# Reordering the opening of an attention-then-FFN kernel, filling TensorE's idle start with products of zeros, and spreading batch 1's attention over the w3 blocks

## The chip, the cores and the metric

The kernel runs on one core of one Trainium2 chip. The metric is the device time of one execution in microseconds (us); lower is better. Profiles are of one execution, and their times count from the start of its span.

## The reference

Eight batches of eight heads, sequence length 576, head width 64. Attention without softmax (cosFormer): rectified queries and keys are multiplied by a cosine and a sine of the position, which makes 128 features of 64 channels; then two products and a division. The result, laid out as 4608 tokens of 512 channels, goes through a feed-forward part with two input products multiplied with each other and two output matrices without a function between them.

```python
def phi(x, c, s):
    r = np.maximum(x, 0.0)
    return np.concatenate([r * c, r * s], axis=-1)
q_p = phi(q, cos_w, sin_w)
k_p = phi(k, cos_w, sin_w)
kv = np.einsum('bhsf,bhsd->bhfd', k_p, v)
z = np.sum(k_p, axis=2)
num = np.einsum('bhsf,bhfd->bhsd', q_p, kv)
den = np.einsum('bhsf,bhf->bhs', q_p, z)[..., None] + 1e-06
x = num / den                    # then laid out as (4608, 512)
...
a = x @ w1
b = x @ w2
h = a * b @ w3
out = h @ w_out
```

## The kernel before

**Attention of one batch.** The 576 positions are held as five chunks: four of 128 rows and one of 64 (`ROWS`). For each chunk `c` of batch `b`:

- `prep_k` and `prep_q` call `features` (L169 and after): VectorE makes the cosine half (L170), ScalarE the sine half (L172), of all eight heads.
- `prep_v` (L184) copies v beside a column of ones into `va`, on VectorE for batches 0 and 1, on POOL (GpSimd) for later ones.
- `q_tr` transposes the query features of the eight heads on TensorE into a PSUM buffer `pst` (L214), and VectorE copies them to `qpT` (L215).
- `kv_chunk` adds the chunk's product of key features and `va` into one PSUM tile (L200). After the fifth chunk ScalarE and VectorE copy one half each to `kvs` (L205, L206).
- `num` multiplies `qpT` by `kvs` (L225); VectorE adds, inverts and multiplies (L229, L230, L232) to give `xblk`.
- `x_tr` transposes `xblk` on TensorE (L251), and ScalarE copies it to `xT` (L252), the input of the FFN.

`num` of batch 0, chunks 0 to 3, uses the pool `ps_first` (two buffers), which is closed before the FFN starts; all later `num` and `kv_chunk` use one buffer, `pnum`. The transposes (`q_tr`, `x_tr`, `w3_tr`) share two `pst` buffers.

**FFN.** Nine tiles `t` of 512 tokens. `ffn_groups(t)` is a generator: sixteen groups of four products with w1 (L291, copied by ScalarE, L294) and w2 (L298, multiplied in by VectorE, L300) in turn, then four output slices of eight products (L305) with `w34b`, copied by ScalarE (L310) and stored by SP (L312). It yields after each w1 or w2 group and twice in each output slice, and after yield `g` the units in `slots[g]` are issued.

**w3 and w_out.** As there is nothing between them, `w34b` = w3 @ w_out is computed once, inside tile 0, in slot 15. For each of eight row blocks `jp`, `w3_tr` transposes a block of w3 (L142); VectorE copies five eighths (L144) and ScalarE, behind it, three (L145) into one of two `w3T` buffers; `w34_mm` makes eight products (L152), and ScalarE copies the result (L154). `w3_tr(jp + 1)` is issued ahead of `w34_mm(jp)`.

**Order.** The schedule is manual: each engine executes its instructions in the order in which the program issues them, and waits at the head of its queue. `spread` deals a list of units evenly over a range of slots. `attention_units(b, done)` gives a batch's attention without the feature part; `done` says how many `q_tr` were issued elsewhere. In slot 15 of tile 0, `extra` puts work of batch 1 behind the named blocks: key features behind block 3, query features behind block 5, three `q_tr` behind block 6, the v copies behind block 7; the rest is spread over slots 16 to 23. Tile 1 carries the features of batches 2 and 3 and the attention of batch 2, and so on.

**Loads.** All loads are issued by POOL in program order at the start: keys of batch 0 (`ks`), queries (`qs`), v (`vs`), w1, w2, w_out, w3 and batch 1 in alternation, batch 2. Batch 3's loads are issued in slot 20 of tile 0 and wait for batch 1's buffers. Each q, k or v load has two halves (L93, L95).

Of the kernel before, what the change touches and what calls it, by code (L numbers as in the profile page):

```python
# [10 lines left out]
FP32 = mybir.dt.float32  # L11
BF16 = mybir.dt.bfloat16
I32 = mybir.dt.int32
ALU = mybir.AluOpType
ACTF = mybir.ActivationFunctionType

P = 128
H, S, D = 8, 576, 64
F = 2 * D
NCH = 5  # L20
# [3 lines left out]
def _trig_tables(nc, pool):  # L24

    s_i = pool.tile([P, NCH], I32, name="s_i")
    nc.gpsimd.iota(s_i[0:64, :], pattern=[[1, 5]], base=0, channel_multiplier=5)
    nc.gpsimd.iota(s_i[64:128, :], pattern=[[1, 5]], base=320, channel_multiplier=4)
    th = pool.tile([P, NCH], FP32, name="th")
    nc.vector.tensor_copy(out=th[:], in_=s_i[:])  # L30
    nc.vector.tensor_scalar_mul(out=th[:], in0=th[:], scalar1=math.pi / 2 / S)
    t2 = pool.tile([P, NCH], FP32, name="t2")
    nc.vector.tensor_mul(out=t2[:], in0=th[:], in1=th[:])

    def poly(outt, coefs):
        nc.vector.tensor_scalar_mul(out=outt[:], in0=t2[:], scalar1=float(coefs[0]))
        for c in coefs[1:-1]:
            nc.vector.scalar_tensor_tensor(out=outt[:], in0=outt[:], scalar=float(c), in1=t2[:],
                                           op0=ALU.add, op1=ALU.mult)

    cosv = pool.tile([P, NCH], FP32, name="cosv")
    poly(cosv, [-1 / 3628800, 1 / 40320, -1 / 720, 1 / 24, -1 / 2, 1.0])
    nc.vector.tensor_scalar_add(out=cosv[:], in0=cosv[:], scalar1=1.0)
    sinv = pool.tile([P, NCH], FP32, name="sinv")
    poly(sinv, [-1 / 39916800, 1 / 362880, -1 / 5040, 1 / 120, -1 / 6, 1.0])
    nc.vector.scalar_tensor_tensor(out=sinv[:], in0=sinv[:], scalar=1.0, in1=th[:],
                                   op0=ALU.add, op1=ALU.mult)
    return cosv, sinv
# [3 lines left out]
def kernel(  # L52
# [11 lines left out]
    nc = tc.nc  # L64
# [6 lines left out]
    const = ctx.enter_context(tc.tile_pool(name="const", bufs=1))  # L71
# [9 lines left out]
    ps_first = first.enter_context(tc.tile_pool(name="ps_first", bufs=2, space=bass.MemoryType.PSUM))  # L81
# [7 lines left out]
    def load(b, which):  # L89
        for name in which:  # L90
            src = {"k": k, "v": v, "q": q}[name]
            t = ld.tile([P, H, NCH, D], BF16, name=name + "s")
            nc.gpsimd.dma_start(out=t[0:64, :, :, :].rearrange("p h j d -> p h (j d)"),  # L93
                                in_=src[b, :, 0:320, :].rearrange("h (p j) d -> p h (j d)", j=5))
            nc.gpsimd.dma_start(out=t[64:128, :, 0:4, :].rearrange("p h j d -> p h (j d)"),  # L95
                                in_=src[b, :, 320:S, :].rearrange("h (p j) d -> p h (j d)", j=4))
            raw[b, name] = t
# [10 lines left out]
        nc.gpsimd.dma_start(out=w3b[:, jp, :], in_=moe_w3[ts(jp, P), :])  # L108

    load(0, "k")  # L110
    cosv, sinv = _trig_tables(nc, const)
    load(0, "q")
    identb = const.tile([P, P], BF16, name="identb")
# [45 lines left out]
    def feat_of(b):  # L159
        if b not in feat:  # L160
            feat[b] = (
                phi.tile([P, NCH, H, F], BF16, name="kp"),
                phi.tile([P, NCH, H, F], BF16, name="qp"),
                va_bufs[b % 2],
            )
        return feat[b]

    def features(dst, src, c):
        R = ROWS[c]  # L169
        nc.vector.tensor_scalar(out=dst[:R, c, :, 0:D], in0=src[:R, :, c, :], scalar1=0.0,  # L170
                                scalar2=cosv[:R, c:c + 1], op0=ALU.max, op1=ALU.mult)
        nc.scalar.activation(out=dst[:R, c, :, D:F], in_=src[:R, :, c, :], func=ACTF.Relu,  # L172
                             scale=sinv[:R, c:c + 1], bias=0.0)

    def prep_k(b, c):
        features(feat_of(b)[0], raw[b, "k"], c)

    def prep_q(b, c):
        features(feat_of(b)[1], raw[b, "q"], c)

    def prep_v(b, c):
        R = ROWS[c]
        eng = nc.vector if b < 2 else nc.gpsimd
        eng.tensor_copy(out=feat_of(b)[2][:R, c, :, 0:D], in_=raw[b, "v"][:R, :, c, :])  # L184
# [3 lines left out]
    def att_of(b):  # L188
        if b not in att:
            att[b] = {"qpT": phi.tile([P, H, S], BF16, name="qpT"), "x": {}}  # L190
        return att[b]

    def kv_chunk(b, c):
        R = ROWS[c]
        kp, qp, va = feat[b]
        if c == 0:
            att_of(b)["kv"] = ps_att.tile([P, 2, 512], FP32, name="pnum")
        kvt = att[b]["kv"]
        for h in range(H):
            nc.tensor.matmul(kvt[:, h // 4, ds((h % 4) * 65, 65)], lhsT=kp[:R, c, h, :],  # L200
                             rhs=va[:R, c, h, 0:D + 1], start=(c == 0 and h % 4 == 0),
                             stop=(c == NCH - 1 and h % 4 == 3))
        if c == NCH - 1:
            kvs = sm.tile([P, H, D + 1], BF16, name="kvs")
            nc.scalar.copy(out=kvs[:, 0:4, :], in_=kvt[:, 0, 0:260])  # L205
            nc.vector.tensor_copy(out=kvs[:, 4:8, :], in_=kvt[:, 1, 0:260])  # L206
            att[b]["kvs"] = kvs

    def q_tr(b, c):
        R = ROWS[c]  # L210
        qp = feat[b][1]
        pst = ps_tr.tile([P, 8, 128], BF16, name="pst")
        for h in range(H):
            nc.tensor.transpose(pst[:, h, 0:R], qp[:R, c, h, :], identb[:R, :R])  # L214
        nc.vector.tensor_copy(out=att_of(b)["qpT"][:, :, ds(128 * c, R)], in_=pst[:, :, 0:R])  # L215
# [38 lines left out]
    def attention_units(b, done=0):  # L254

        order = [0, 1, 2, 3, 4] if b % 2 == 0 else [4, 0, 1, 2, 3]
        u = [(lambda c=c: kv_chunk(b, c)) for c in range(NCH)]
        if done < 1:
            u.insert(2, lambda: q_tr(b, order[0]))
        if done < 2:  # L260
            u.insert(len(u) - 1, lambda: q_tr(b, order[1]))
        for i in range(NCH + 1):
            if i < NCH:
                u.append(lambda c=order[i]: num(b, c))
            if max(done, i + 2) == i + 2 < NCH:
                u.append(lambda c=order[i + 2]: q_tr(b, c))
            if i >= 1:
                u.append(lambda c=order[i - 1]: x_tr(b, c))
        return u
# [46 lines left out]
    def prep_units(b):  # L316
        return [(lambda f=f, c=c: f(b, c)) for f in (prep_k, prep_v, prep_q) for c in range(NCH)]

    def spread(units, first, last, slots):
        for i, u in enumerate(units):  # L320
            slots[min(last, first + int(i * (last + 1 - first) / len(units)))].append(u)
# [3 lines left out]
        prep_k(0, c)  # L325
    for c in range(NCH):
        prep_q(0, c)
        q_tr(0, c)
    for c in range(NCH):
        prep_v(0, c)  # L330
        kv_chunk(0, c)
    for c in range(4):
        num(0, c)
# [6 lines left out]
    for t in range(NT):  # L340
        slots = [[] for _ in range(24)]
        if t == 0:
            slots[1].append(lambda: num(0, 4))
            slots[3].append(lambda: x_tr(0, 4))
            slots[14].append(lambda: w3_tr(0))
            w = slots[15]
            extra = {
                3: [(lambda c=c: prep_k(1, c)) for c in range(NCH)],
                5: [(lambda c=c: prep_q(1, c)) for c in range(NCH)],
                6: [(lambda c=c: q_tr(1, c)) for c in (4, 0, 1)],  # L350
                7: [(lambda c=c: prep_v(1, c)) for c in range(NCH)],
            }
            for jp in range(8):
                if jp < 7:
                    w.append(lambda jp=jp: w3_tr(jp + 1))
                w.append(lambda jp=jp: w34_mm(jp))
                w += extra.get(jp, [])
            slots[20].append(lambda: load(3, "kvq"))
            spread(attention_units(1, 3), 16, 23, slots)
        elif t == 1:  # L360
            spread(prep_units(2), 0, 6, slots)
            spread(attention_units(2), 4, 22, slots)
            slots[8].append(lambda: load(4, "kvq"))
            spread(prep_units(3), 9, 22, slots)
        else:
            if t + 3 < B:
                load(t + 3, "kvq")
            if t + 2 < B:
                spread(prep_units(t + 2), 0, 22, slots)
            if t + 1 < B:  # L370
                spread(attention_units(t + 1), 0, 22, slots)
        for g, _ in enumerate(ffn_groups(t)):
            for u in slots[g]:
                u()
# [30 lines left out]
```

## Time and profile before

| | |
|---|---|
| median of 3 runs | 295.59 us (295.51 to 295.9) |
| the profiled execution | 295.17 us, of which the span is 293.4 |
| TensorE busy | 264.0 us (90% of the span), 2112 products |
| VectorE busy | 148.9 us (51%) |
| ScalarE busy | 143.7 us (49%) |
| POOL busy | 61.1 us (21%) |
| granted TensorE clock in the records | 1.000 |

In rows of the timeline, the columns are start, duration, engine, line, operation, output <- input, shape and count; in brackets the idle time of the engine before it and what ended it. PE is TensorE, PEld its weight load, DVE VectorE, ACT ScalarE. Products overlap one another in the pipeline, so a group's pace is read better from the chain (start, duration, what), where each piece ends when the next begins.

### The profile page before, as it was taken

How to read it: one execution, taken by the hardware profiler on the slowest of the kernel's cores; microseconds unless marked ns; L12 is line 12 of the kernel's file. 1: busy time of each engine (PE TensorE's matmuls, PEld its weight loads, DVE VectorE, ACT ScalarE, POOL GpSimd, SP SyncE). 2: the span in 40 equal slices, each digit the busy share in tenths (PEclk: the TensorE clock that was granted, in tenths of full speed). 3: DMA queues.
4: the chain of work that ended last, by engine and by line, in shares of the span. 5: the costliest groups of instructions: out<-in, count | busy, mean ns of one | idle time of the engine just before them, and what ended most of it. 6: DMA issues, size and time to landing. Idle time of an engine off the chain costs nothing.

```text
span 293.4 us, 5335 instructions
## 1 busy us (share of the span) xinstructions
PE 264.0 (90%) x2112; PEld 142.8 (49%) x2112; DVE 148.9 (51%) x355; ACT 143.7 (49%) x253; POOL 61.1 (21%) x101
## 2 busy tenths in 40 slices
PE   0147899979899999999999999999999999999993
PEld 0136345535545555555555555555555555444441
DVE  3446334334747963774576377736742762430320
ACT  0901333592277767448536752774473235333331
POOL 8631442024206325301430450000000000000000
PEclk9999999999999999999999999999999999999999
DMA  7999999963939899493875650140033004106005
GB/s 96 196 202 208 205 201 203 134 77 40 201 72 132 112 137 205 82 126 91 135 93 80 117 100 2 37 110 0 2 73 73 0 3 111 33 2 143 0 18 127
DMA packets 36489, 29.18 MB, mean 99 GB/s; under 512 B 2160, under 2 KB 30832, under 8 KB 36464
## 3 DMA queue, kind: packets, MB, share of 16 engines
q0 software_dynamic: 30704, 19.40, 47.6%
q1 hardware_dynamic: 5760, 9.44, 12.8%
q8 instruction: 16, 0.26, 0.4%
q14 instruction: 9, 0.07, 0.1%
HBM read 38.80 MB, written 9.44 MB: 164 GB/s over the span
## 4 chain that ended last, share of the span: by engine, by line
PE 82%; ACT 6%; DVE 4%; DMA 4%; issue 2%; POOL 1%; ACTq 0%; POOLq 0%
PE ffnps L305 21%; PE ffnps L298 20%; PE ffnps L291 20%; PE pst L214 6%; PE pnum L200 4%; PE pnum L225 4%; PE ffnps L152 3%; ACT kp L172 3%; PE pst L251 3%; DMA vs<-in_v_dram 2%; DMA ks<-in_k_dram 2%; DVE xblk L232 1%; ACT qp L172 1%; DVE qpT L215 1%; PE pst L142 1%
## 5 line engine op out<-in xcount | busy, mean ns | idle before, releaser
L300 DVE TENSOR_TENSOR abT<-asb,ffnps 128x512 bf16<-128x512 bf16 x72 | 49.3, 685 | 78.5 <-PE ffnps L298 69.8
L294 ACT CAST asb<-ffnps 128x512 bf16<-128x512 f32 x72 | 42.1, 586 | 75.9 <-PE ffnps L291 75.8
L291 PE MATMUL ffnps<-xT,w1b 128*128 128x512 bf16 x288 | 74.7, 382 | 1.1 <-ACT xT L252 1.1
L298 PE MATMUL ffnps<-xT,w2b 128*128 128x512 bf16 x288 | 74.3, 380 | 0.0
L305 PE MATMUL ffnps<-w34b,abT 128*128 128x512 bf16 x288 | 70.9, 379 | 0.0
L214 PE MATMUL pst<-identb,qp 128*128 128x128 bf16 (+1 forms) x320 | 24.5, 223 | 19.0 <-ACT qp L172 14.4
L291 PEld LDWEIGHTS <-w1b 128*128 128x128 bf16 x288 | 26.2, 98 | 26.7 <-issue 2.0
L305 PEld LDWEIGHTS <-abT 128*128 128x128 bf16 x288 | 25.6, 98 | 23.8 <-DVE abT L300 0.2
L298 PEld LDWEIGHTS <-w2b 128*128 128x128 bf16 x288 | 25.2, 98 | 24.2 <-issue 0.6
L310 ACT COPY osb<-ffnps 128x512 f32<-128x512 f32 x36 | 21.1, 586 | 31.2 <-PE ffnps L305 26.5
L214 PEld LDWEIGHTS <-qp 128*128 128x128 bf16 (+1 forms) x320 | 20.1, 102 | 29.2 <-ACT qp L172 16.8
L215 DVE COPY qpT<-pst 128x1024 bf16<-128x1024 bf16 (+1 forms) x40 | 25.2, 632 | 12.3 <-PE pst L214 12.1
L252 ACT COPY xT<-pst 128x512 bf16<-128x512 bf16 (+1 forms) x40 | 21.6, 543 | 12.6 <-PE pst L251 11.7
L172 ACT ACTIVATE qp<-qs,sinv 128x512 bf16<-128x512 bf16 (+1 forms) x40 | 27.1, 718 | 0.0
L172 ACT ACTIVATE kp<-ks,sinv 128x512 bf16<-128x512 bf16 (+1 forms) x40 | 26.9, 717 | 0.0
L232 DVE TENSOR_TENSOR xblk<-pnum,den 128x512 bf16<-128x512 f32 (+1 forms) x36 | 24.8, 689 | 1.2
L225 PEld LDWEIGHTS <-qpT 128*128 128x128 bf16 (+1 forms) x320 | 15.5, 104 | 12.2 <-issue 3.0
L200 PEld LDWEIGHTS <-kp 128*128 128x128 bf16 (+1 forms) x320 | 14.9, 101 | 9.4 <-issue 3.2
L184 POOL COPY va<-vs 128x512 bf16<-128x512 bf16 (+1 forms) x30 | 17.4, 639 | 2.4 <-PE pnum L200 2.4
L200 PE MATMUL pnum<-va,kp 128*128 128x65 bf16 (+1 forms) x320 | 16.6, 199 | 0.7 <-DVE va L184 0.7
L251 PEld LDWEIGHTS <-xblk 128*128 128x128 bf16 (+1 forms) x160 | 11.3, 101 | 11.9 <-DVE xblk L232 2.7
L251 PE MATMUL pst<-identb,xblk 128*128 128x128 bf16 (+1 forms) x160 | 15.6, 223 | 1.5 <-DVE xblk L232 1.2
(47 smaller groups left out, 163.9 us busy)
## 6 DMA issues: line engine op xcount, KB each, us to landing
out_dram<-osb SPq DMA_DIRECT2D x72, 128.0 KB, 2.4
ks<-in_k_dram POOLq DMA_DIRECT2D x8, 320.0 KB, 4.7
qs<-in_q_dram POOLq DMA_DIRECT2D x8, 320.0 KB, 6.3
vs<-in_v_dram POOLq DMA_DIRECT2D x8, 320.0 KB, 7.0
ks<-in_k_dram POOLq DMA_DIRECT2D x8, 256.0 KB, 5.4
qs<-in_q_dram POOLq DMA_DIRECT2D x8, 256.0 KB, 7.0
vs<-in_v_dram POOLq DMA_DIRECT2D x8, 256.0 KB, 8.1
w3b<-in_moe_w_dram POOLq DMA_DIRECT2D x8, 256.0 KB, 15.5
```

The lines of the kernel that those rows point to most:

```text
L172: nc.scalar.activation(out=dst[:R, c, :, D:F], in_=src[:R, :, c, :], func=ACTF.Relu, scale=sinv[:R, c:c + 1], bias=0.0)
L200: nc.tensor.matmul(kvt[:, h // 4, ds((h % 4) * 65, 65)], lhsT=kp[:R, c, h, :], rhs=va[:R, c, h, 0:D + 1], start=(c == 0 and h % 4 == 0), s ...
L214: nc.tensor.transpose(pst[:, h, 0:R], qp[:R, c, h, :], identb[:R, :R])
L215: nc.vector.tensor_copy(out=att_of(b)["qpT"][:, :, ds(128 * c, R)], in_=pst[:, :, 0:R])
L225: nc.tensor.matmul(nt[:R, h // 4, ds((h % 4) * 65, 65)], lhsT=qpT[:, h, ds(128 * c, R)], rhs=kvs[:, h, :], start=True, stop=True)
L232: nc.vector.tensor_tensor(out=xblk[:R], in0=n4[:, :, :, 0:D], in1=den[:R].unsqueeze(3).to_broadcast([R, 2, 4, D]), op=ALU.mult)
L251: nc.tensor.transpose(pst[:, kc, 0:R], xf[:, ts(kc, 128)], identb[:R, :R])
L291: nc.tensor.matmul(aT[:, :], lhsT=w1b[:, kc, ts(jc, 128)], rhs=x[:, kc, :], start=(kc == 0), stop=(kc == 3))
L294: nc.scalar.copy(out=asb[:], in_=aT[:, :])
L298: nc.tensor.matmul(bT[:, :], lhsT=w2b[:, kc, ts(jc, 128)], rhs=x[:, kc, :], start=(kc == 0), stop=(kc == 3))
L300: nc.vector.tensor_mul(out=abT[:, jc, :], in0=asb[:], in1=bT[:, :])
L305: nc.tensor.matmul(ops[:, :], lhsT=abT[:, jc, ts(ms, 128)], rhs=w34b[:, jc, :], start=(jc == 0), stop=(jc == 7))
```

## The change

1. Right after the load of batch 0's keys, VectorE sets a tile of zeros, ScalarE does one Relu on a single column of it, and TensorE does 32 products of 128x512 of these zeros into a `ps_first` buffer that nothing reads.
2. In the opening, the five `prep_q` of batch 0 are issued together, and only then `q_tr` and `prep_v` alternate; the five `kv_chunk` follow.
3. In slot 15 of tile 0, key features of batch 1 stand behind block 1, query features behind block 2, the v copies behind block 3, and the first ten units of the attention (all five `kv_chunk`, three `q_tr`, two `num`) behind blocks 4 to 7. The other ten units are spread over slots 16 to 23.

```diff
     load(0, "k")
+    zeros = const.tile([P, 512], BF16, name="zeros")
+    nc.vector.memset(zeros[:], 0.0)
+    tiny = const.tile([P, 1], FP32, name="tiny")
+    nc.scalar.activation(out=tiny[:], in_=zeros[:, 0:1], func=ACTF.Relu, scale=1.0, bias=0.0)
+
+    def idle_mms(n):
+
+        w = ps_first.tile([P, 2, 512], FP32, name="pfirst")
+        for _ in range(n):
+            nc.tensor.matmul(w[:, 0, :], lhsT=zeros[:, 0:128], rhs=zeros[:], start=True, stop=True)
+
+    idle_mms(32)
     cosv, sinv = _trig_tables(nc, const)
...
         prep_q(0, c)
+    for c in range(NCH):
         q_tr(0, c)
+        prep_v(0, c)
     for c in range(NCH):
-        prep_v(0, c)
         kv_chunk(0, c)
...
+            att1 = attention_units(1)
             extra = {
-                3: [(lambda c=c: prep_k(1, c)) for c in range(NCH)],
-                5: [(lambda c=c: prep_q(1, c)) for c in range(NCH)],
-                6: [(lambda c=c: q_tr(1, c)) for c in (4, 0, 1)],
-                7: [(lambda c=c: prep_v(1, c)) for c in range(NCH)],
+                1: [(lambda c=c: prep_k(1, c)) for c in range(NCH)],
+                2: [(lambda c=c: prep_q(1, c)) for c in range(NCH)],
+                3: [(lambda c=c: prep_v(1, c)) for c in range(NCH)],
+                4: att1[0:3],
+                5: att1[3:6],
+                6: att1[6:8],
+                7: att1[8:10],
             }
...
-            spread(attention_units(1, 3), 16, 23, slots)
+            spread(att1[10:], 16, 23, slots)
```

## The prediction

> **What bounds the kernel now.** I read the page's busy shares first, then the chain that ended last, then the timeline of the opening and of the stage in which w3 is folded into w_out, and last the reasons for TensorE's idle time there.
>
> ```profile
> span 293.4 us, 5335 instructions
> PE 264.0 (90%) x2112; PEld 142.8 (49%) x2112; DVE 148.9 (51%) x355; ACT 143.7 (49%) x253; POOL 61.1 (21%) x101
> PE 82%; ACT 6%; DVE 4%; DMA 4%; issue 2%; POOL 1%; ACTq 0%; POOLq 0%
> ```
>
> The third row is the chain: TensorE is 82% of it. So the amount of TensorE work sets the time, and a change of order can win only what TensorE now idles, plus what it runs at a slow pace. Both lie in two places. The first is the opening (timeline):
>
> ```profile
> 7.23 1.28 ACT L172 ACT_TABLE_LOAD   x1 [7.23 <-DMA ks<-in_k_dram]
> 8.53 3.17 ACT L172 ACTIVATE kp<-ks,sinv 128x512 bf16<-128x512 bf16 x5
> 10.88 0.35 DVE L170 TENSOR_SCALAR qp<-qs,cosv 128x512 bf16<-128x512 bf16 x1 [1.82 <-DMA qs<-in_q_dram]
> 11.60 3.15 ACT L172 ACTIVATE qp<-qs,sinv 128x512 bf16<-128x512 bf16 x5
> 12.36 1.03 PE L214 MATMUL pst<-identb,qp 128*128 128x128 bf16 x8 [12.36 <-ACT qp L172]
> 13.43 0.69 DVE L215 COPY qpT<-pst 128x1024 bf16<-128x1024 bf16 x1 [2.21 <-PE pst L214]
> ...
> 14.33 0.56 POOL L108 DMA_DIRECT2D w3b<-in_moe_w_dram  x1 [0.76 <-DMA vs<-in_v_dram]
> 14.53 1.01 PE L214 MATMUL pst<-identb,qp 128*128 128x128 bf16 x8 [1.14 <-DVE qp L170]
> ...
> 21.58 0.42 DVE L215 COPY qpT<-pst 128x512 bf16<-128x512 bf16 x1 [0.77 <-PE pst L214]
> 21.93 1.25 DVE L184 COPY va<-vs 128x512 bf16<-128x512 bf16 x5
> 22.26 2.47 PE L200 MATMUL pnum<-va,kp 128*128 128x65 bf16 x40 [0.71 <-DVE va L184]
> 24.77 0.38 ACT L205 CAST kvs<-pnum 128x260 bf16<-128x260 f32 x1 [10.01 <-PE pnum L200]
> ...
> 31.86 1.86 PE L291 MATMUL ffnps<-xT,w1b 128*128 128x512 bf16 x4 [0.67 <-ACT xT L252]
> ```
>
> The reader is to see a ring. Chunk 1's transposes (14.53) wait for a VectorE feature product, which sits behind the copy of chunk 0, which waits for chunk 0's transposes. One turn takes 14.53 - 12.36 = 2.17 us, although no resource is full. The first FFN product comes at 31.86. The second place is the w3 stage (timeline):
>
> ```profile
> 52.55 0.59 ACT L154 CAST w34b<-ffnps 128x512 bf16<-128x512 f32 x1 [0.65 <-PE ffnps L152]
> ...
> 57.38 3.17 ACT L172 ACTIVATE kp<-ks,sinv 128x512 bf16<-128x512 bf16 x5
> 60.45 0.46 ACT L145 COPY w3T<-pst 128x384 bf16<-128x384 bf16 x1
> 60.81 0.58 ACT L154 CAST w34b<-ffnps 128x512 bf16<-128x512 f32 x1
> 60.96 0.82 PE L152 MATMUL ffnps<-woutb,w3T 128*128 128x512 bf16 x3 [0.41 <-ACT w3T L145]
> 62.30 3.17 ACT L172 ACTIVATE qp<-qs,sinv 128x512 bf16<-128x512 bf16 x5
> 65.53 1.52 PE L214 MATMUL pst<-identb,qp 64*128 64x64 bf16 x24 [1.57 <-ACT qp L172]
> 71.92 0.38 ACT L205 CAST kvs<-pnum 128x260 bf16<-128x260 f32 x1
> 72.32 0.43 DVE L206 CAST kvs<-pnum 128x260 bf16<-128x260 f32 x1 [3.50 <-ACT kvs L205]
> ...
> 74.42 0.43 PE L225 MATMUL pnum<-kvs,qpT 128*128 128x65 bf16 x8 [1.20 <-DVE xblk L232]
> ```
>
> ScalarE's feature blocks (3.17 us) hold back its part of the w3T copies, so TensorE stands at 60.96 and 65.53; later it stands for the single pnum buffer (74.42). The pieces of dense TensorE work, from the chain:
>
> ```profile
> 33.72 1.10 PE ffnps L298 x4
> ...
> 39.95 0.86 PE ffnps L298 x4
> ...
> 50.34 0.45 PE pst L142 x8
> 50.79 1.73 PE ffnps L152 x8
> ...
> 69.64 0.76 PE pnum L200 x24
> ...
> 76.17 0.22 PE pst L251 x4
> ...
> 77.35 0.26 PE pnum L225 x8
> ...
> 83.12 1.04 PE ffnps L291 x4
> ```
>
> After 50.79 + 1.73 = 52.52 (second w34 block done) and before tile 1 starts at 83.12 there are 5 x 0.45 (w3 transposes), 6 x 1.73 (w34), 8 x 0.86 (output products) and about 5.7 us of attention (five chunks each of 0.76/3, 0.45, 0.26 and 0.22, less something for the chunk of 64 rows): 25.2 us in 30.6. The idle 5.4 us are the most that this stage can give.
>
> **The change, part by part.**
>
> *Feature order.* ScalarE's table load leaves the path, since the tiny Relu now triggers it before the keys land at 7.23; ScalarE's kp then ends near 10.4 instead of 11.7, and its first qp starts when the queries are there (VectorE's row: 10.88) and ends near 11.6. Its later four follow every 0.61 us. VectorE does all five qp from 10.88 to about 12.4 (0.3 each). TensorE's transposes of chunk 0 run 11.65 to 12.7 and the copies can start at 12.72. The copy of chunk 0 ends at 13.4. Then comes the added wait: prep_v of chunk 0 needs both halves of vs. The row at 14.33, a POOL issue released by vs, shows that the second half landed just before it, at about 14.1. Queued behind that wait are the copies of chunks 1 to 4, and behind them, through the two pst buffers, TensorE's transposes of chunks 3 and 4: 0.7 us lost. From 14.1 VectorE runs full: 1.25 for the v copies, 3 x 0.66 + 0.42 for the qpT copies, 3.7 us with gaps: 17.8. TensorE keeps up: a chunk's transposes take 1.03 after the copy that frees their buffer, two copies ahead. The first four kv chunks are finished by then, and the last costs 2.47/5 = 0.5 and some 0.15 to the end: 18.5. Before, that point is 24.77. Gain 6.2. What follows up to the first FFN product (24.77 to 31.86, 7.1 us of num, normalise, transpose) is not changed in order, so that product comes near 25.6. Bounds: 6.9 if the v wait costs nothing, 5.2 if VectorE's copies each lose 0.2 to the interleaving. Memset and Relu lie beside the wait for the keys: nothing, and without that cover under 2 us together.
>
> *Idle products.* 32 products of 128x512. The row at 31.86 gives 1.86/4 = 0.465 each at the slow pace, that at 39.95 0.215 at the full one: 6.9 to 14.9 us in all. They start after VectorE's memset; no row shows when VectorE may begin (its first instruction waited for POOL). POOL's first DMA at 1.25 and a copy's 0.69 give 0.5 to 2.0, so their end lies between 7.4 and 16.9. The pace changed within 2 us of dense work at 31.86 to 33.7, but 2.47 us of kv products at 22.26 were not enough. I take a change after about 5 us: 11 slow (5.1) and 21 fast (4.5), end near 11, before the transposes at 11.65: nothing lost. At the upper end the transposes start at 16.9.
>
> *What the idle products give.* Kept fast to the FFN, the clock would save 2.96 - 1.73 = 1.2 on the first eight products (1.86 and 1.10 against 0.86 each), and in the head:
>
> ```profile
> 27.67 0.65 PE L225 MATMUL pfirst<-kvs,qpT 128*128 128x65 bf16 x8
> 30.58 0.61 PE L251 MATMUL pst<-identb,xblk 128*128 128x128 bf16 x4 [0.43 <-DVE xblk L232]
> 78.98 0.42 PE L225 MATMUL pnum<-kvs,qpT 128*128 128x65 bf16 x8
> 80.10 0.39 PE L251 MATMUL pst<-identb,xblk 128*128 128x128 bf16 x4
> ```
>
> 0.2 on each of two num and one transpose on the path, 0.1 in the last kv chunk: 0.7. The price is 0 to 1.9. Between the idle products and the FFN lie 14 us of broken work like that of 12 to 32 now, which ran slow throughout; that is the nearest row, so I take 0. The Trainium skill (TensorE: Matmul & The Clock Gate, Part 1) says that the gate opens after a busy window of some 3.4 us and closes after an idle one, and Part 4 that transposes do not count as busy in the same way; by the two together the gate would have closed by 17 and the sum would be mine, while by Part 1 alone, with no fully idle window, it would be the rival's 1.9 better. No row here shows a gate closing.
>
> *w3 stage.* The work is the same; kp and qp of batch 1 move to blocks 1 and 2. I follow it on the old clock from 52.51. ScalarE: w34b(1) 52.55, kp 53.03 to 56.20, w3T(3) to 56.56, w34b(2), qp 56.94 to 60.11, w3T(4) to 60.47. TensorE: w34(3) stops after five products at 56.22 and goes on at 56.61; w34(4) stops at 58.79 and goes on at 60.52: 2.1 us of standing, as much as now (0.4 and 1.6). Then kv 0, 1 and a transposition, to 62.0; block 5 to 64.18, kv 2, 3 and q_tr 0 to 65.15, block 6 to 67.33, kv 4 to 67.6. Here a wait is added: num of chunk 4 stands right behind kv 4, and kvs takes ScalarE's w34b(6) (0.59), then 0.38 and 0.43: num at 68.76, 1.2 us idle with w34(7) queued behind it. Today 0.86 of an output product covers most of that. w34(7) ends at 70.8 and now covers the normalisation, so the 1.20 at 74.42 goes. The remaining ten units spread over eight slots; num 3 waits 0.2 for pnum. Tile 1 starts at 81.56 instead of 83.12. Gain 1.5; bounds: -1 if the two feature blocks in a row cost as much again as one stop, 1.6 (plus copies), and 3.3 if they cost nothing.
>
> *Transfers.*
>
> ```profile
> 46.64 0.68 POOL L95 DMA_DIRECT2D qs<-in_q_dram  x1 [0.66 <-DMA vs<-in_v_dram]
> ...
> 60.84 0.82 POOL L93 DMA_DIRECT2D ks<-in_k_dram  x1 [13.52 <-ACT kp L172]
> ```
>
> POOL's last issue for batch 2 (46.64) waited for v of batch 1, so v is in by then, and keys and queries, issued ahead of it, before. With the shift of 6.2 the keys are wanted at 47, queries and v later: hidden. Batch 3's keys, issued at 60.84 once kp has read the buffer, go out some 10 us earlier, still behind batch 2's loads, which tile 1 wants. On SP nothing moves. Free; without this cover a late load would cost its lateness.
>
> *Sum.* The profiled execution took 295.17 (span 293.4 and 1.8 around it), 0.4 below the median. 295.17 - 6.2 - 1.5 = 287.5. From tile 1 on order and work are unchanged: 0, within 1 either way, as its idle pieces fall otherwise on POOL's copies.
>
> **The rivals.** *The clock stays open:* 287.5 - 1.9 = 285.6. For it: no gap of the new head is longer than the 1.6 us that the full pace survived before 65.53. Against: the head's low density.
> *The w3 stage gives nothing or loses 1:* 289.0 to 290. For it: ScalarE's two blocks now come without the w3T work between them that today's order has; against: the standing worked out is no longer.
> *The idle products stay slow:* transposes at 16.9, kv ends some 6.1 later at 23.0, head gain 1.8: 291.9.
> *Slower:* the same queue, one step further: the idle products sit ahead of everything on TensorE. If they began only when the keys land (7.2) and stayed slow they would end at 22.1, kv at 28.2, 3.4 later than now: 295.17 + 3.4 - 1.5 = 297.1. It decides from an end at 20. Against: nothing but a memset stands before them.
> *No effect:* the head would have to hang on a transfer that no order moves. vs is that transfer, but it is in 7 us before va is wanted now: about 295.2 if it is not.
>
> **How the numbers follow.** My case 0.46, the open clock 0.32, the weak w3 stage 0.12, slow idle products 0.06, slower 0.02, no effect 0.02. My case's own range, with the bounds of the head (-0.7, +1) and tile 1, is 286.3 to 288.7; with the open clock below and the weak w3 stage above it is 284.7 to 290.0, and some 0.14 lie outside. A difference under 0.2% (0.6 us) cannot be told from none. Faster 0.96, same 0.02, slower 0.02.
>
> **What would show it.** The copies of qpT and va alternating on VectorE from 12.7 to about 17.8, with one wait for vs; kv's end near 18.5; the first FFN product near 25.6 and whether its four take 1.86 or 0.86; idle products ending before 11.6; TensorE standing once for 1.7 us behind w3T(4) and once for 1.2 before num of chunk 4; tile 1's first product 7.7 us earlier. I am wrong if the transposes wait for idle products, if VectorE's ring persists, or if the w3 standing grows.

## The result and the profile after

The changed kernel takes 288.66 us (median of 4 runs, 288.4 to 289.04) against 295.75 (4 runs, 295.51 to 296.04): the ratio is 0.9761, with a 95% interval of 0.9744 to 0.9778. The forecast was 287.5, between 284.7 and 290.0. The profiled execution took 288.88 us. One execution of `order_only`, below, took 697.51 us, more than twice as long as the others, and is left out of its figures.

First the page of the changed kernel: span, the engines' busy row, the granted clock in 40 slices, and the chain's shares by engine.

```profile
span 287.1 us, 5398 instructions
PE 270.8 (94%) x2144; PEld 143.8 (50%) x2144; DVE 149.8 (52%) x356; ACT 144.0 (50%) x254; POOL 61.0 (21%) x101
PEclk9995999889999999999999999999999999999999
PE 73%; DMA 15%; ACT 5%; POOL 3%; DVE 2%; issue 1%; POOLq 0%; ACTq 0%
```

The clock row of the kernel before:

```profile
PEclk9999999999999999999999999999999999999999
```

The clock row is the news: a half-rate slice near 25 us, and two reduced ones between 50 and 65. It was 9 throughout before. The 15% of DMA in the chain are a trap: the chain comes to ScalarE's key features (46.31) by a transfer of batch 1's keys (to 36.14) and one of w3 (to 46.28). In the timeline ScalarE starts them right behind its w34b copy of 45.83, VectorE has read the same keys from 44.58 on, and w3_dealt, below, runs the first of ScalarE's at 44.0. So they did not wait for a transfer.

The timeline of the opening:

```profile
1.20 8.61 PE L120 MATMUL pfirst<-zeros 128*128 128x512 bf16 x32 [1.20 <-DVE zeros L112]
...
7.25 3.17 ACT L184 ACTIVATE kp<-ks,sinv 128x512 bf16<-128x512 bf16 x5 [5.01 <-DMA ks<-in_k_dram]
10.97 1.53 DVE L182 TENSOR_SCALAR qp<-qs,cosv 128x512 bf16<-128x512 bf16 x5 [1.91 <-DMA qs<-in_q_dram]
11.73 1.23 PE L226 MATMUL pst<-identb,qp 128*128 128x128 bf16 x16 [1.93 <-ACT qp L184]
...
13.91 0.29 DVE L196 COPY va<-vs 128x512 bf16<-128x512 bf16 x1 [0.80 <-DMA vs<-in_v_dram]
14.12 0.68 DVE L227 COPY qpT<-pst 128x1024 bf16<-128x1024 bf16 x1
...
15.97 1.61 PE L212 MATMUL pnum<-va,kp 128*128 128x65 bf16 x40
16.85 0.27 DVE L196 COPY va<-vs 64x512 bf16<-64x512 bf16 x1
17.63 0.38 ACT L217 CAST kvs<-pnum 128x260 bf16<-128x260 f32 x1 [3.50 <-PE pnum L212]
24.42 1.87 PE L303 MATMUL ffnps<-xT,w1b 128*128 128x512 bf16 x4 [0.67 <-ACT xT L264]
26.08 1.91 PE L310 MATMUL ffnps<-xT,w2b 128*128 128x512 bf16 x4
28.41 1.04 PE L303 MATMUL ffnps<-xT,w1b 128*128 128x512 bf16 x4
```

The ring is gone: the v copies and the copies of qpT follow one another from 13.91 to 17.12 behind one wait for vs. The 40 kv products take 1.61 us (2.47 before), so they ran at the fast pace; the first FFN products do not (1.87 and 1.91 for four). "The gate" is short here for the granted clock: open is the full clock (1.00), closed is half of it (0.50). Half-microsecond windows show where it moved. A row has the window, its length, the busy times of PE, PEld, DVE, ACT and POOL, and then the clock, third from the end:

```profile
21.00:21.50 0.50, 0.43 (x9) 0.44 (x10) 0.43 (x4) 0.05 (x1) 0.00 (x0) 0.90 1.25 205
28.00:28.50 0.50, 0.50 (x9) 0.46 (x10) 0.40 (x1) 0.00 (x0) 0.00 (x0) 0.78 1.19 211
55.50:56.00 0.50, 0.50 (x7) 0.50 (x8) 0.42 (x1) 0.00 (x0) 0.50 (x2) 0.53 1.43 195
58.50:59.00 0.50, 0.50 (x3) 0.15 (x1) 0.00 (x0) 0.00 (x0) 0.00 (x0) 0.56 1.32 181
```

A mean of 0.90 over half a microsecond that starts at 1 and ends at 0.5 puts the closing at 21.40; in the same way it opened at 28.22, closed at 55.53 and opened at 58.94. The second closing lies in the w3 stage:

```profile
49.90 0.82 PE L164 MATMUL ffnps<-woutb,w3T 128*128 128x512 bf16 x3 [0.41 <-ACT w3T L157]
...
53.81 0.82 PE L164 MATMUL ffnps<-woutb,w3T 128*128 128x512 bf16 x3 [1.57 <-ACT w3T L157]
...
56.17 3.26 PE L164 MATMUL ffnps<-woutb,w3T 128*128 128x512 bf16 x8
...
63.98 0.42 PE L237 MATMUL pnum<-kvs,qpT 128*64 128x65 bf16 x8 [1.06 <-DVE kvs L218]
...
76.87 1.03 PE L303 MATMUL ffnps<-xT,w1b 128*128 128x512 bf16 x4
```

The two stops for w3T (0.41, 1.57) and the stop for kvs (1.06) are there as worked out, and one block of eight products takes 3.26 instead of 1.89.

From the timelines of all profiles, the milestones that the next section uses (us). "w34" is the start of ScalarE's copy of the second w34 block, and the last two columns are the stretches between.

| kernel | kvs copy | first FFN product | w34 | tile 1 | first FFN to w34 | w34 to tile 1 |
|---|---|---|---|---|---|---|
| before | 24.77 | 31.86 | 52.55 | 83.12 | 20.69 | 30.57 |
| after | 17.63 | 24.42 | 45.83 | 76.87 | 21.41 | 31.04 |
| order_only | 17.98 | 24.78 | 46.51 | 77.08 | 21.73 | 30.57 |
| no_idle | 18.12 | 24.91 | 46.69 | 76.06 | 21.78 | 29.37 |
| w3_old | 17.25 | 24.04 | 45.60 | 76.18 | 21.56 | 30.58 |
| fill_head | 17.19 | 23.80 | 43.41 | 72.77 | 19.61 | 29.36 |
| w3_dealt | 17.62 | 24.62 | 45.73 | 72.78 | 21.11 | 27.05 |
| w3_fill | 18.44 | 25.52 | 47.66 | 77.03 | 22.14 | 29.37 |
| fill_dealt_num | 18.11 | 24.72 | 44.34 | 70.39 | 19.62 | 26.05 |
| idle72 | 24.04 | 31.04 | 51.73 | 81.09 | 20.69 | 29.36 |
| fill_noidle | 17.82 | 24.43 | 44.04 | 73.41 | 19.61 | 29.37 |
| no_relu | 17.99 | 24.78 | 46.23 | 75.59 | 21.45 | 29.36 |
| steady | 17.33 | 23.94 | 43.55 | 69.60 | 19.61 | 26.05 |

Before to after: 7.44 won up to the first FFN product, 0.72 lost up to w34, 0.47 lost up to tile 1, and nothing from there on: 6.25, which is the change of the span (293.4 to 287.1).

### The profile page after: what moved, and what is told of

The parts are those of the page before. It is cut to its first block, busy times and chain, and to the rows that moved or that the text cites. A ratio compares the mean times of both kernels' runs of the same rounds, so it can differ in the third digit from the quotient of the medians.

```text
span 287.1 us, 5398 instructions
## 1 busy us (share of the span) xinstructions
PE 270.8 (94%) x2144; PEld 143.8 (50%) x2144; DVE 149.8 (52%) x356; ACT 144.0 (50%) x254; POOL 61.0 (21%) x101
## 4 chain that ended last, share of the span: by engine, by line
PE 73%; DMA 15%; ACT 5%; POOL 3%; DVE 2%; issue 1%; POOLq 0%; ACTq 0%
PE ffnps L317 22%; PE ffnps L310 18%; PE ffnps L303 17%; DMA ks<-in_k_dram 6%; PE pst L226 5%; DMA w2b<-in_moe_w_dram 4%; PE pnum L237 3%; DMA w3b<-in_moe_w_dram 3%; PE pnum L212 3%; PE ffnps L164 3%; PE pst L263 3%; ACT kp L184 2%; DMA vs<-in_v_dram 2%; ACT qp L184 1%; DVE kp L182 1%
## 5 line engine op out<-in xcount | busy, mean ns | idle before, releaser
L264 ACT COPY xT<-pst 128x512 bf16<-128x512 bf16 (+1 forms) x40 | 21.7, 543 | 14.9 <-PE pst L263 14.1
L226 PE MATMUL pst<-identb,qp 128*128 128x128 bf16 (+1 forms) x320 | 22.7, 213 | 3.9 <-ACT qp L184 2.4
L226 PEld LDWEIGHTS <-qp 128*128 128x128 bf16 (+1 forms) x320 | 19.0, 97 | 14.0 <-ACT qp L184 3.7
L164 PE MATMUL ffnps<-woutb,w3T 128*128 128x512 bf16 x64 | 16.8, 405 | 2.0 <-ACT w3T L157 2.0
L212 PEld LDWEIGHTS <-kp 128*128 128x128 bf16 (+1 forms) x320 | 14.0, 97 | 9.0 <-issue 3.1
L182 DVE TENSOR_SCALAR kp<-ks,cosv 128x512 bf16<-128x512 bf16 (+1 forms) x40 | 17.1, 459 | 0.6 <-DMA ks<-in_k_dram 0.6
```

The costliest lines, as they stand in the source:

```text
L164: nc.tensor.matmul(acc[:, :], lhsT=w3T[:, lc, :], rhs=woutb[:, lc, :], start=(lc == 0), stop=(lc == 7))
```

## The experiments

Each edit is against the changed kernel, unless it says otherwise; none changes what is computed.

**The order of the opening alone** (against the kernel before).

```diff
+    for c in range(NCH):
         q_tr(0, c)
+        prep_v(0, c)
     for c in range(NCH):
-        prep_v(0, c)
         kv_chunk(0, c)
```

> The kernel before with part 2 of the change alone (feature products together, then transposes and v copies in turn). If the ring on VectorE was what cost the opening: kv's end near 18.3 instead of 24.77 (the wait for vs to 13.9, then 4.3 us of copies, then a kv chunk at the slow pace), the first FFN product near 25.4, its first four products at 0.465 each as before, and 295.7 - 6.4 = 289.3 us. If the rival holds that the fast clock of the idle products made most of the opening's gain, the transposes at the slow pace hold VectorE back and kv ends after 20: 291 or more.

289.12 us (median of the other five executions), ratio 0.9764 (0.9745 to 0.9784): as much as the whole change gains. kvs is reached at 17.98, but not in the expected way. TensorE's rows:

```profile
12.39 4.00 PE L214 MATMUL pst<-identb,qp 128*128 128x128 bf16 x40 [12.39 <-DVE qp L170]
16.32 1.62 PE L200 MATMUL pnum<-va,kp 128*128 128x65 bf16 x40
```

The transposes now stand close together for 4 us, and the kv products behind them take 1.62, the fast pace: with no product of zeros the transposes alone had opened the gate. It closed at 22.5, and the FFN started slow (20.69 became 21.73). The mean clocks of the five executions are alike (0.984 to 0.988), so the profiled one (0.985) is not an exception.

**Without the 32 products.** `idle_mms(32)` is taken out.

> The changed kernel without the 32 products of zeros; memset and Relu stay. The clock theory: the gate closes at 21.45 in the changed kernel anyway, so that its FFN starts slow and even keeps the slow pace longer (8 products in 3.66 us against 2.96 in the kernel before). Without the idle products the opening loses 0.7 us up to the first FFN product (num and transposes at the slow pace) and gets about that back when the gate opens earlier in the FFN: 288.7, within 0.5. Rival: the idle products carry 1 to 2 us of the gain: 289.7 or more.

289.09 us, 0.9745 (0.972 to 0.9769): within the interval of the changed kernel. The 32 products by themselves bring nothing that can be measured; the gate they open closes again before the FFN. (Up to the FFN they bring 0.5: 24.91 against 24.42.) This kernel has two kinds of execution: the profiled one (288.06) and one more (287.51) have mean clocks of 0.987 and 0.986, the other three 0.999 and 289.1 to 289.5. So its row in the table is that of a faster one; a gate that first opens in the FFN, as in the kernel before, would fit the three, but none of them was profiled.

**The old w3 stage in the changed kernel.** `extra` and the spread of `attention_units(1, 3)` as before.

> The changed kernel with the w3 stage of the kernel before (features of batch 1 behind blocks 3 and 5, three transposes behind 6, v behind 7). Between the end of the second w34 block and the start of tile 1 lie 31.08 us in the changed kernel and 30.61 before. Theory: this part is a loss of 0.5, since the gate closes from 55.5 to 58.6 after two stops of TensorE; with the old order the gate stays open and the time is 288.2. Rival (the prediction's sum): the stage is a gain of 1.5, and undoing it gives 290.2.

288.41 us, 0.9748 (0.9722 to 0.9774): the same as the changed kernel. The table says why neither theory was right. The new stage takes 29.37, 1.20 less than the old one's 30.57, in six profiles in which the gate stays open in it; in the changed kernel's own profile the gate closes, and it takes 31.04. So the part is a gain of 1.2 that one closing (1.67) more than eats. The old order is not free of closings either: two of the six executions of `w3_old` have mean clocks of 0.974 and 0.976 and took 289.5 and 290.2, the others 0.984 to 0.988 and 287.8 to 288.6.

**Zeros where the gate closes.** Fifteen more products of zeros, into the free pnum buffer, in TensorE's gaps between 18 and 24; `fill(n)` issues n of them.

```diff
         num(0, c)
         if c >= 1:
+            fill((0, 4, 2, 2)[c])
             x_tr(0, c - 1)
+    fill(3)
     x_tr(0, 3)
+    fill(4)
```

> The changed kernel with 15 more products of zeros in the gaps of TensorE between num and transposes of batch 0 (4, 2, 2, 3 ahead of the four transposes of xblk, 4 ahead of the first FFN product), written to the free pnum buffer. If the gate closes at 21.45 because TensorE is too little busy in the 3.4 us or so before, it now stays open, the first eight FFN products take 1.73 instead of 3.66, and the time is 288.66 - 1.9 - 0.1 = 286.7. Rival: products of zeros do not hold the gate, or they push the transposes back by as much: 288.7 or more.

285.12 us, 0.9624 (0.9606 to 0.9643), more than expected. The rows of TensorE:

```profile
21.12 0.59 PE L129 MATMUL pnum<-zeros 128*128 128x512 bf16 x2
...
23.80 1.03 PE L311 MATMUL ffnps<-xT,w1b 128*128 128x512 bf16 x4
25.99 1.04 PE L311 MATMUL ffnps<-xT,w1b 128*128 128x512 bf16 x4
```

The first four FFN products take 1.03, and the stretch to w34 is 19.61 (21.41): 1.80. The opening is 0.6 shorter, and the w3 stage had no closing in this execution (1.68). All four executions have mean clocks of 0.996 to 1.000, like those of the kernel before, whose profile shows no closing; by an estimate from the span one closed stretch of 3.41 us takes off 0.006.

**Only the 15, not the 32.** `fill_head` without `idle_mms(32)`.

> The changed kernel without its 32 products of zeros at the start, but with the 15 in the gaps between num and transposes of batch 0 (with both: 285.12; without both: 289.09). In the kernel without the 32 the transposes, dense from 12.1 to 16.4, opened the gate by themselves in the profiled execution, and it closed at 22.6. Theory: what counts is that TensorE is busy from 18 to 24, so the 15 are worth most of it: 285.7, with more spread, since in some executions the gate is not open by 16.4. Rival: without the early 32 the gate is not open in time, the 15 run slow and push the transposes back: 289 or more.

286.68 us, 0.9679 (0.9646 to 0.9712), from 285.4 to 288.8, between the two expectations. In the profiled execution (283.6 us of span) the stretch is as good as with both, 19.61. Where the zeros stand counts for more than how many there are. That the slower executions (287.4 to 288.8) are those in which the gate opens late is the theory, and it is not shown: the profiled one is the fastest.

**72 instead of 32**, for the rival in which the result is slower.

> The changed kernel with 72 products of zeros instead of 32. They end near 18.4 (8 slow ones to 4.5, 64 at 0.217) instead of 9.8, and the first transposes stand behind them. The rival for a slower result put the point of no gain at an end of 20. By the same sum kv ends near 24, 6.4 later than in the changed kernel, and the time is 295.0. If TensorE's queue let the transposes pass: 288.7.

293.72 us, 0.9922 (0.9896 to 0.9947). kvs is at 24.04, as summed up, and the time is 1.3 less than expected; the w3 stage had no closing in its profile (29.36). The products end at 19.25 with 2.2 us still won, so by an estimate that adds the two the point of no gain lies near an end of 21.4, against 20 in the prediction.

```profile
1.20 18.05 PE L120 MATMUL pfirst<-zeros 128*128 128x512 bf16 x71 [1.20 <-DVE zeros L112]
24.04 0.38 ACT L217 CAST kvs<-pnum 128x260 bf16<-128x260 f32 x1 [10.09 <-PE pnum L212]
```

**Without the early Relu.** The activation on `tiny` is taken out.

> The changed kernel without the early Relu, so that the table load falls behind the keys' landing again. ScalarE's first query feature then ends at 12.3 instead of 11.7, and the copy of chunk 0 at 13.8 instead of 13.1; the wait for vs, to 13.9, hides that: 288.7. Rival (the whole chain moves): 289.3.

287.59 us, 0.9715 (0.969 to 0.9739). No loss: the table load is hidden. VectorE still waits 0.24 for vs before its first v copy; kvs is 0.36 later (17.99) because vs itself was (14.27 against 13.91). That it is faster than the changed kernel goes with the clock: its w3 stage had no closing (29.36), four of its five executions have mean clocks of 0.985 to 0.987, and the fifth, at 0.970, took 289.4; the changed kernel's have 0.974 to 0.982. Whether the edit has a part in that is not shown.

**Features dealt out.**

```diff
-                1: [(lambda c=c: prep_k(1, c)) for c in range(NCH)],
-                2: [(lambda c=c: prep_q(1, c)) for c in range(NCH)],
-                3: [(lambda c=c: prep_v(1, c)) for c in range(NCH)],
-                4: att1[0:3],
-                5: att1[3:6],
+                0: [(lambda c=c: prep_k(1, c)) for c in (0, 1)],
+                1: [(lambda c=c: prep_k(1, c)) for c in (2, 3)],
+                2: [lambda: prep_k(1, 4), lambda: prep_q(1, 4)],
+                3: [(lambda c=c: prep_v(1, c)) for c in range(NCH)] + [lambda: prep_q(1, 0)],
+                4: [lambda: prep_q(1, 1), lambda: prep_q(1, 2)] + att1[0:3],
+                5: [lambda: prep_q(1, 3)] + att1[3:6],
```

> The changed kernel with the features of batch 1 dealt out two chunks to a block (blocks 0 to 5) instead of five behind block 1 and five behind block 2. ScalarE then has 1.07 + 2 x 0.63 = 2.33 us of work in a block of 2.18 and never 3.17 at once. Theory: TensorE's two stops for w3T (0.41 and 1.57) go, and with them the closing of the gate at 55.5 (1.8): 288.66 - 3.5 = 285.2; without any effect on the gate 286.8. Rival: the features only move the wait to kv or to the transposes of the queries, which follow the last features closely: 288 or more.

284.65 us, 0.9616 (0.9594 to 0.9637). The stage takes 27.05: 2.3 less than with the gate open, 4.0 less than in the changed kernel's profile. TensorE goes through the blocks that stopped before:

```profile
48.15 1.89 PE L164 MATMUL ffnps<-woutb,w3T 128*128 128x512 bf16 x8
49.88 0.61 PE L154 MATMUL pst<-identb,w3b 128*128 128x128 bf16 x8
50.33 1.89 PE L164 MATMUL ffnps<-woutb,w3T 128*128 128x512 bf16 x7
```

**Zeros in the stop of the w3 stage.** Seven products ahead of the fifth w34 block.

> The changed kernel with 7 products of zeros (1.5 us at the full pace) ahead of the fifth w34 block, where TensorE stands for 1.57 us behind ScalarE's copy of w3T. The standing stays as long, but TensorE is busy in it. Theory: the stop closes the gate in most runs and costs 1.8 us at half the pace; kept busy, the time is 288.66 - 1.7 = 287.0. Rival: the gate closes for another reason (the transposes after the stop): 288.7, or 0.1 more.

288.02 us, 0.9713 (0.9686 to 0.974), from 286.8 to 289.1: it settles nothing. The stage took 29.37 with the gate open, but so it did in other kernels without these zeros. Its profile shows something else: the same opening as in the changed kernel, but the gate closed at 17.3 and opened at 30.9 (windows):

```profile
17.00:17.50 0.50, 0.50 (x19) 0.50 (x16) 0.50 (x3) 0.00 (x0) 0.49 (x1) 0.79 1.46 199
30.50:31.00 0.50, 0.50 (x3) 0.23 (x2) 0.40 (x1) 0.00 (x0) 0.06 (x1) 0.56 1.13 209
```

So where the gate closes differs between executions: up to there the code is that of the changed kernel.

**Three together:** `fill_head`, `w3_dealt`, and num of chunk 4 moved behind the last w34 block.

```diff
-                6: att1[6:8],
-                7: att1[8:10],
+                6: att1[6:7],
+                7: att1[7:9],
...
-            spread(att1[10:], 16, 23, slots)
+            spread(att1[9:], 16, 23, slots)
```

> The changed kernel with three things together: the 15 products of zeros in the gaps of the opening (alone 285.12), the features dealt out two chunks to a block, and num of chunk 4 moved from right behind the fifth kv chunk to behind the last w34 block, so that this block covers the copies of kvs (1.06 us of standing). If the three costs add up: 285.12 - 0.4 - 1.6 - 1.0 = 282.1. Rival: ScalarE, filled to 2.33 us in each block of 2.18, hands the wait on, and only the 1.0 is gained: 284.1.

282.49 us, 0.9555 (0.9527 to 0.9583). The stage takes 26.05, exactly 1.00 less than `w3_dealt`: the last w34 block covers the copies of kvs.

```profile
57.36 1.90 PE L172 MATMUL ffnps<-woutb,w3T 128*128 128x512 bf16 x8
59.19 0.45 PE L245 MATMUL pnum<-kvs,qpT 128*64 128x65 bf16 x8
```

**Three together and 13 more zeros** (38 at the start, 4 in the wait for v, 3 in the wait for kvs).

> The kernel with 15 products in the opening's gaps, dealt features and the moved num (282.49, with two executions at 283.4 and 284.0), and 13 more products of zeros: 38 instead of 32 at the start, 4 in the wait for v behind the third transposition, 3 in the wait for kvs. Theory: the two slower executions are such in which the gate closed early, near 17 as in the profile of the kernel with 7 products in the w3 stage; kept busy there too, all executions are at 282.0 to 282.5. Rival: the added products delay the transposes and num by as much as they save: 282.5 to 283.5 and the same spread.

282.22 us, 0.9522 (0.9507 to 0.9538), from 281.6 to 282.3: the fastest version, 2.4% below the changed kernel by the two ratios. Against the version before it the median is the same within the intervals; what goes is the spread (it had 282.0 to 284.0). The mean clocks bear the theory out: the two slower executions of the version before, 283.38 and 284.03, have 0.994 and 0.988, which is what one and two closed stretches of 3.41 us would give (an estimate from the span), its others 0.999 or more; here all five have 0.998 or more.

## Why the prediction came out as it did

*The opening (forecast 6.2, measured 7.14 at kvs).* Right in mechanism: the ring on VectorE was the cost, one wait for vs remained (to 13.9; forecast 14.1), and order_only shows that this part alone gains as much as the whole change. The term was too small by 0.9: the wait for vs ended 0.2 earlier; VectorE's run of copies took 3.2 (13.91 to 17.12) and not 3.7, as a turn of copy and v copy took 0.80 (14.12 to 14.92) against some 0.9 assumed; and the last kv chunk ran at the fast pace and took 0.51 to kvs, where 0.65 was priced by a row of the shut gate.

*The idle products (forecast: end near 11, nothing lost).* Right: they end at 9.8, the change of pace after 3.3 us.

*What they give (forecast 0 of a possible 1.9).* Near in the sum (0.30 won from kvs to the first FFN product, 0.72 lost from there to w34), wrong in the reason. I took the density of the old opening as the nearest row and expected it to stay slow. Compressed, the new opening opens the gate without help in order_only's profile and holds it to 21 or 22 in most profiles (17.3 in that of w3_fill); then num, VectorE's division and the transposes leave TensorE idle, and it closes 3 us ahead of the FFN. The rival's condition, that no window be fully idle, held, and it closed all the same: in the 3.41 us ahead of 21.40 TensorE was busy for 1.83. Then the FFN pays more than before: from its first product to VectorE's first multiplication behind the eighth it takes 3.68 (24.42 to 28.10), 3.07 before (31.86 to 34.93). fill_head shows that most of the rival's 1.9 was there to be had, by zeros in another place: against the kernel before, 0.48 from kvs to the first FFN product (6.61 against 7.09) and 1.08 from there to w34 (19.61 against 20.69).

*The w3 stage (forecast 1.5, measured -0.47 in the profile).* This step failed. The standing was right: the stops for w3T and kvs were 0.41, 1.57 and 1.06 against 0.4, 1.7 and 1.2, and with the gate open the stage gains 1.20. Missing was the gate: I treated a stop as costing its length. In one profile of seven with this order, half-rate products after the stop cost another 1.67. It was not one unlucky execution, either: two closed stretches of 3.41, as in the openings of six other profiles, go with mean clocks of 0.984 to 0.988, and the four executions of the changed kernel have 0.974 to 0.982. By that reading the gate was closed for longer in each of them; where, only the profiled one shows.

Why it closed there and not in the other six is open. In order_only and w3_old a window of 3.41 us, laid out from the closing in the opening (22.53 and 21.46, each plus ten windows), holds a stop of 1.57 whole (57.91 to 59.48, 57.01 to 58.58), and the gate stayed open; in no_relu and idle72, which have the new order, the window that starts nine lengths after the closing does the same. How busy TensorE is in a window tells a part. The last window before each of the nine closings (in eight profiles) has TensorE busy for 1.60 to 1.89 us of its 3.41, and none that was busier ended in a closing. The window with the stop has 1.84 in the changed kernel, which closed, and 1.79 to 1.85 in the four that did not. So the stop stands at an edge that these figures do not resolve. The products of zeros in the stop did not tell it apart either.

*From tile 1 on (forecast 0):* 0.0.

*The sum.* The profiles show 6.25 won where 7.7 was forecast: 0.94 more at kvs and 0.30 more up to the FFN, 0.72 less up to w34 and 1.97 less in the w3 stage. That the time came within 1.2 us of the forecast is in part luck, as errors of opposite sign made up for one another.

## What to carry to other kernels

Look for rings: an instruction that waits in an in-order queue behind a copy which waits for the work that the instruction feeds; reordering one queue undid this one, which gained as much as the whole change. Cost a stop of TensorE as its length plus what the clock may lose behind it, and read the clock in windows of half a microsecond, since a whole-run mean of 0.98 does not say where it fell. Work of the right size per turn (two features a block, 2.33 us beside 2.18) beat the same work in lumps by 2.3 us, before the clock is counted.

## What the hardware showed that was not expected

The gate's times are multiples of one length. It stayed closed for 6.82 us (21.40 to 28.22) and 3.41 (55.53 to 58.94) in the changed kernel and 13.65 (17.29 to 30.94) in w3_fill: 2, 1 and 4 times 3.41. In the six other profiles with a closing it stayed closed for 6.82 or 6.83. The Trainium skill (TensorE: Matmul & The Clock Gate, Part 1) gives a free-running window of 3413 ns; the runs agree. Its Part 4 says that the full rate does not engage for transposes. Here it did: 40 transposes over 4.00 us were followed by kv products at 1.62 instead of 2.47 in order_only, with nothing else on TensorE before. (The rows show products with the identity matrix; in which mode TensorE ran them no row shows.)

The clock in the records starts at 1.00 whatever the pace is. In these windows of the changed kernel the first eight products of zeros take 3.26 us, half the pace of the next, and both rows show 1.00; the FFN's slow start in the kernel before was hidden by this as well.

```profile
1.20:4.46 3.26, 3.26 (x8) 1.18 (x9) 1.10 (x6) 1.03 (x2) 3.09 (x6) 1.00 0.55 54
4.46:9.81 5.35, 5.34 (x25) 2.25 (x23) 3.51 (x17) 2.56 (x5) 4.92 (x10) 1.00 1.39 193
```
